# Completing and scaling a softmax sum on VectorE, in front of its reciprocal, in place of GpSimd

## The chip, the cores and the metric

The kernel runs on one core of a Trainium2 chip. A core has TensorE (PE in the profile, with its weight loads as PEld), VectorE (DVE), ScalarE (ACT), GpSimd (POOL) and SyncE (SP), which here only issues transfers. The metric is the device time of one execution in microseconds (us), the median of several runs. The trace is that of one profiled execution, and its times are counted from the start of its span.

## The reference

Attention over 8 batches of 12 heads, 448 positions and 64 features, and then a two-layer network on its output. What is computed:

```python
q_n, k_n = (rmsnorm(q, g_q), rmsnorm(k, g_k))
scores = scale * np.matmul(q_n, k_n.transpose(0, 1, 3, 2))
scores = scores - np.max(scores, axis=-1, keepdims=True)
attn = np.exp(scores)
attn = attn / (np.sum(attn, axis=-1, keepdims=True) + 1e-09)
attn_out = np.matmul(attn, v)
...
x = np.ascontiguousarray(attn_out.transpose(0, 2, 1, 3)).reshape(B * S, H * D)
h = x @ w_in
g = np.where(h > 0.0, h, alpha * (np.exp(np.minimum(h, 0.0)) - 1.0))
return (g @ w_out).astype(np.float32)
```

The network's weights, 768 x 2048 and 2048 x 768, arrive as 64-bit floats.

## The kernel before

**Attention.** Two heads make a pair, and there are 48 pairs. A pair has 7 tiles of 128 query rows (2 x 448 rows), so there are 336 tiles T. A tile goes through these steps: `s_mm` (L488) multiplies queries with keys into one of four PSUM banks; `s_max` (L495, VectorE) takes the negated maximum of each row; `s_exp` (L501, ScalarE) takes the exponential in place and adds the row up, the sum being written by a second, short instruction; `s_z` (L505, GpSimd) adds 1e-9 to the sum and multiplies it by 2^-7; `s_rec` (L512, VectorE) takes its reciprocal; `s_hi` (L516, ScalarE) scales the exponentials and writes them as 16-bit numbers; `s_lo` (L522, VectorE, two instructions) subtracts these from the scaled exponentials and writes what is left as 16-bit numbers too; `s_tr` (L533) issues the transfer that transposes both. Maximum, sum and reciprocal lie side by side in a small tile `st` of 128 x 3, of which there are six. `attend` (L544) multiplies a finished pair with its values into a bank of its own (`av`), and `x_high` and `x_low` (L551, L555) bring the result to SBUF as two 16-bit halves, one 128-row block of the network's input.

**Preparing q, k and v.** Each pair's q and k are loaded, squared (L327), summed (L331), their roots refined on small tiles (L335 to L346), multiplied by them on GpSimd (L356), split into two 16-bit halves (L367 to L388) and transposed by transfers (L396). Values are scaled and split on GpSimd (L402 to L414).

**Weights.** `conv` takes the 64-bit weights apart on the chip: a load (L187), two ScalarE instructions on the upper and lower words (L194, L195), a shift on VectorE (L198), an addition on GpSimd (L204), column sums on TensorE (L115) whose maximum VectorE reads (L118) and turns into powers of two (L124), and a sign put in by VectorE (L223). The first matrix then takes L246 to L260 (GpSimd's part is L249, TensorE's L256 and L257), the second L280 to L292 (GpSimd's are L280 and L289, ScalarE's L285). The first matrix is converted from the start on, the second from half step 60 on. From the eighth piece of the second matrix on its column sums use the bank `av`.

**The network.** `mlp` multiplies a batch by the first matrix (L630), applies the activation (L568 on ScalarE, L571 on GpSimd, L577 on VectorE, and L582 and L585, which split the result into two halves), multiplies by the second (L644), and writes the result out. Every product is made of three 16-bit products.

**The order.** Everything is emitted in half steps h by a loop written out by hand, and each engine runs its instructions in that order. An odd half step has `s_exp(T)`, `s_rec(T-1)` and `s_lo(T-2)`, an even one `s_max(T)`, `s_z(T-1)`, `s_hi(T-2)` and transposes; a table `tasks` adds the other steps at half steps of their own. From half step 92 on (the first batch's 84 and 8 more) 6.9 matrix products of the network are emitted in each half step, between the attention's; up to there TensorE has attention and weights alone. Transfers are all issued from SP's queue in the same order.

Of the kernel before, what the change touches and what calls it, by code (L numbers as in the profile page):

```python
# [14 lines left out]
ALU = mybir.AluOpType  # L15
# [17 lines left out]
def tile_attention_then_elu_mlp(ctx: ExitStack, tc: tile.TileContext, qk, v, v_scan, gg, w_in, w_out, out):  # L33
# [13 lines left out]
    nc = tc.nc  # L47
# [15 lines left out]
    def t_mo():  # L63
# [8 lines left out]
        out=neg, in0=ident, scalar1=-1.0, scalar2=None, op0=ALU.mult  # L72
# [3 lines left out]
        out=ident, in0=ident, scalar1=2.0**UP, scalar2=None, op0=ALU.mult  # L76
# [224 lines left out]
    nat, vn, vt, qkt, pts, pss, p16s, stats = ({} for _ in range(8))  # L301
# [179 lines left out]
    def s_mm(T):  # L481
        p, j = divmod(T, NJ)
        ps = pss[T] = t_s()
        qq = qkt[p].rearrange("p t j n -> p t (j n)")
        for t in (1, 2):
            for h, r0, q0, n in cuts(ORDER[j]):
                lhs = qq[:, 0, h * S + q0 : h * S + q0 + n]
                nc.tensor.matmul(  # L488
                    ps[r0 : r0 + n, :S], lhs, qq[:, t, h * S : h * S + S],
                    start=(t == 1), stop=(t == 2),  # L490
                )

    def s_max(T):
        st = stats[T] = small("st", 3, bufs=6)
        nc.vector.tensor_reduce(  # L495
            out=st[:, 0:1], in_=pss[T][:, :S], axis=AX.X, op=ALU.max, negate=True
        )

    def s_exp(T):
        ps, st = pss[T][:, :S], stats[T]  # L500
        nc.scalar.activation(ps, ps, AF.Exp, bias=st[:, 0:1], accum_out=st[:, 1:2])  # L501

    def s_z(T):
        st = stats[T]
        nc.gpsimd.tensor_scalar(  # L505
            out=st[:, 1:2], in0=st[:, 1:2], scalar1=1e-9, scalar2=2.0**-7, op0=ALU.add, op1=ALU.mult
        )

    def s_rec(T):

        st = stats[T]
        nc.vector.reciprocal(out=st[:, 2:3], in_=st[:, 1:2])  # L512

    def s_hi(T):
        p16 = p16s[T] = pool.tile([128, 2 * S], F16, tag="p16", name="p16", bufs=3)
        nc.scalar.activation(p16[:, :S], pss[T][:, :S], AF.Copy, scale=stats[T][:, 2:3])  # L516

    def s_lo(T):

        p16, ps, r = p16s[T], pss.pop(T), stats.pop(T)[:, 2:3]  # L520
        for o, a, z in ((S + 64, 0, 384), (S, 384, S)):
            nc.vector.scalar_tensor_tensor(  # L522
                out=p16[:, o : o + z - a], in0=ps[:, a:z], scalar=r, in1=p16[:, a:z],
                op0=ALU.mult, op1=ALU.subtract,
            )

    def s_tr(T):
        p, j = divmod(T, NJ)
        p16 = p16s.pop(T)
        for h, r0, q0, n in cuts(ORDER[j]):  # L530
            if 2 * p + h not in pts:
                pts[2 * p + h] = pool.tile([128, NJ, S], F16, tag="pt", name="pt", bufs=2)
            nc.sync.dma_start_transpose(  # L533
                out=pts[2 * p + h][:, :, q0 : q0 + n], in_=p16[r0 : r0 + n, :]
            )

    def attend(p):


        pt = [pts.pop(2 * p), pts.pop(2 * p + 1)]  # L540
        terms = [(j, i) for j in range(4) for i in (0, 1)] + [(j, 0) for j in range(4, NJ)]
        for k, (j, i) in enumerate(terms):
            for h in (0, 1):
                nc.tensor.matmul(  # L544
                    av[64 * h : 64 * h + 64, :S], vt[p][:, j % 4, h, i],
                    pt[h][:, j, :], start=(k == 0), stop=(k == len(terms) - 1),
                )
        del vt[p]
# [109 lines left out]
    def steps_at(h, steps):  # L658
        for i, s in steps:
            at(h + i, s)  # L660

    def run_tasks(h, kind):
        for fn, args in tasks.get(h, []):
            if kind == (0 if fn in (load_qk, load_v, scan_load) else 2 if fn in late else 1):
                fn(*args)
# [54 lines left out]
    for h in range(H0, LAST):  # L720
        T, odd = divmod(h, 2)
        run_tasks(h, 0)
        ok = lambda t: 0 <= t < NCHUNK
        if odd:
            if ok(T):
                s_exp(T)
            if ok(T - 1):
                s_rec(T - 1)
            if ok(T - 2):
                s_lo(T - 2)  # L730
        else:
            if ok(T):
                s_max(T)
            if ok(T - 1):
                s_z(T - 1)
            if ok(T - 2):
                s_hi(T - 2)

            for t in (T - 4, T - 3):
                if ok(t) and (t % NJ == 0) == (t == T - 4):  # L740
                    s_tr(t)
        run_tasks(h, 1)
        want = int(max(0, (h + 1 - START)) * RATE)
        n = max(0, want - done)
        mm = []
        p, r = divmod(h, HP)

        if ok(T + 1) and odd == (h >= START):
            mm.append(lambda: s_mm(T + 1))
        if r == 7 and 0 <= p - 1 < NP:  # L750
            mm = [lambda mm=mm: (*(fn() for fn in mm), attend(p - 1))]
        parts = len(mm) + 1
        for k in range(parts):
            for _ in range(n * (k + 1) // parts - n * k // parts):
                r = next(moe, None)
                done += 1
                if r:
                    steps_at(h + 1, enumerate(r))
            if k < len(mm):
                mm[k]()  # L760
        run_tasks(h, 2)
# [50 lines left out]
```

## Time and profile before

| | us |
|---|---|
| median of 3 runs | 1323.66 (1322.05 to 1326.17) |
| the profiled execution | 1321.52 |
| its span | 1319.7 |
| PE busy | 1202.7 (91%) |
| DVE busy | 897.0 (68%) |
| ACT busy | 820.8 (62%) |
| POOL busy | 672.4 (51%) |
| the sum's completion, L505 on POOL, 336 times | 78.6, 234 ns each on average |
| the reciprocal, L512 on DVE, 336 times | 51.5, 153 ns each on average |

Busy times are those of an engine's own instructions; waiting is not part of them. In a timeline a row gives the start, the duration, the engine, the line, the operation, what it writes and reads, and in square brackets how long the engine had been idle before it and who released it. Consecutive instructions of one engine can overlap a little, as reading, computing and writing are pipelined. In a list of waits a row names who waited, for whom, how long in total, how often, and the longest.

### The profile page before, as it was taken

The page shows a single profiled execution, that of the slowest core. Times are in us where ns is not written, and L with a number is a line of the kernel's source. Part 1 is how long each engine was busy: PE and PEld are TensorE (multiplying, and loading weights), DVE is VectorE, ACT ScalarE, POOL GpSimd, SP SyncE. Part 2 cuts the span into 40 slices and gives each one's busy share as a digit, 9 for nine tenths or more (in the row PEclk, how much of TensorE's full clock was granted, in tenths as well). Part 3 has the DMA queues.
Part 4 walks back from the last instruction along what each step waited for, and adds up shares of the span by engine and source line. Part 5 has one row for each costly group of instructions (what it writes and reads, how often), then busy time and mean ns, then how long its engine had stood idle before and what let it go on. Part 6 is the DMA issues. An engine that isn't in the chain of part 4 may idle for free.

```text
span 1319.7 us, 22020 instructions
## 1 busy us (share of the span) xinstructions
PE 1202.7 (91%) x6976; PEld 723.1 (55%) x6976; DVE 897.0 (68%) x2257; ACT 820.8 (62%) x1761; POOL 672.4 (51%) x915
## 2 busy tenths in 40 slices
PE   3665558879999999999999999999999999999998
PEld 1322224436755675566655765577556755666576
DVE  7776788988668756885588657865687568842310
ACT  5767767776667657675577657756676567742310
POOL 5776798888445544544455345543454445421100
PEclk9777768989999999999999999999999999999999
DMA  7899998879878787888878877879687877764011
GB/s 236 195 233 223 201 203 189 209 205 204 199 140 194 163 187 151 178 165 189 173 153 177 190 172 147 187 171 193 144 190 163 189 150 154 152 135 110 1 46 60
DMA packets 491013, 221.76 MB, mean 168 GB/s; under 512 B 451856, under 2 KB 467344, under 8 KB 490896
## 3 DMA queue, kind: packets, MB, share of 16 engines
q1 hardware_dynamic: 490896, 220.35, 75.6%
q8 instruction: 55, 0.90, 0.3%
q14 instruction: 62, 0.51, 0.1%
HBM read 96.01 MB, written 14.16 MB: 83 GB/s over the span
## 4 chain that ended last, share of the span: by engine, by line
PE 67%; DMA 4%; DVE 4%; POOL 2%; issue 2%; ACT 2%; SPq 0%; ACTq 0%; POOLq 0%
PE mo L644 32%; PE mo L630 22%; PE s L488 7%; PE av L544 6%; DMA pt<-p 2%; DMA vscan<-in_v_scan 1%; DVE p L522 1%; POOL e L571 1%; POOL t L381 1%; DVE st L495 1%; DVE mv L139 0%; DVE e L577 0%; ACT p L516 0%; DVE wts L198 0%; ACT t L367 0%
## 5 line engine op out<-in xcount | busy, mean ns | idle before, releaser
L630 PE MATMUL mo<-x,whi 128*128 128x448 f16 x1536 | 425.8, 354 | 1.5 <-DVE e L577 1.5
L644 PE MATMUL mo<-g,who 128*128 128x448 f16 x1536 | 422.5, 352 | 0.0
L495 DVE TENSOR_REDUCE st<-s 128x1 f32<-128x448 f32 x336 | 208.1, 619 | 205.5 <-PE s L488 205.3
L522 DVE SCALAR_TENSOR_TENSOR p<-s,st,p 128x384 f16<-128x384 f32 (+1 forms) x672 | 266.4, 437 | 34.7 <-ACT p L516 33.2
L516 ACT ACTIVATE p<-s,st 128x448 f16<-128x448 f32 x336 | 213.1, 634 | 120.7 <-DMA pt<-p 95.3
L644 PE MATMUL mo<-g,wls 128*128 128x448 f16 x768 | 272.0, 354 | 0.0
L630 PE MATMUL mo<-x,wli 128*128 128x448 f16 x768 | 271.8, 354 | 0.0
L644 PEld LDWEIGHTS <-who 128*128 128x128 f16 x1536 | 221.9, 144 | 72.3
L505 POOL TENSOR_SCALAR st<-st 128x1 f32<-128x1 f32 x336 | 78.6, 234 | 350.7 <-ACT s L501 333.5
L501 ACT ACTIVATE s<-s,st 128x448 f32<-128x448 f32 x336 | 203.8, 607 | 74.0 <-DVE st L495 64.6
L488 PE MATMUL s<-qkt 128*128 128x448 f16 (+1 forms) x768 | 191.4, 372 | 58.9 <-DVE p L522 30.7
L630 PEld LDWEIGHTS <-whi 128*128 128x128 f16 x1536 | 150.6, 98 | 139.6 <-issue 4.4
L571 POOL TENSOR_SCALAR e<-e,isc 128x448 f32<-128x448 f32 x128 | 94.1, 735 | 179.5 <-ACT e L568 177.7
L644 PEld LDWEIGHTS <-wls 128*128 128x128 f16 x768 | 111.5, 145 | 42.1 <-issue 7.5
L488 PEld LDWEIGHTS <-qkt 128*128 128x128 f16 (+1 forms) x768 | 61.3, 102 | 131.6 <-DVE p L522 52.2
L544 PE MATMUL av<-pt,vt 128*64 128x448 f16 x1056 | 114.6, 366 | 5.2 <-DVE mx L118 4.3
L585 DVE SCALAR_TENSOR_TENSOR g<-e,gsc,g 128x448 f16<-128x448 f32 x128 | 100.8, 788 | 24.4 <-ACT g L582 24.3
L630 PEld LDWEIGHTS <-wli 128*128 128x128 f16 x768 | 75.2, 98 | 74.5 <-issue 8.1
L582 ACT ACTIVATE g<-e,gsc 128x448 f16<-128x448 f32 x128 | 85.4, 667 | 44.9 <-DVE e L577 44.1
L568 ACT ACTIVATE e<-mo,sc 128x448 f32<-128x448 f32 x128 | 80.4, 628 | 52.3 <-PE mo L630 33.1
L381 POOL TENSOR_TENSOR t<-nat,t 128x896 f16<-128x896 f32 x48 | 92.7, 1931 | 4.8 <-ACT t L367 1.1
L577 DVE SCALAR_TENSOR_TENSOR e<-e,mo 128x448 f32<-128x448 f32 x128 | 78.2, 611 | 23.9 <-POOL e L571 19.3
(84 smaller groups left out, 1330.0 us busy)
## 6 DMA issues: line engine op xcount, KB each, us to landing
wls<-wl_d SPq DMA_DIRECT2D x48, 512.0 KB, 3.9
nat<-in_qk SPq DMA_DIRECT2D x48, 448.0 KB, 3.7
raws<-in_w_in SPq DMA_DIRECT2D x16, 768.0 KB, 5.5
vn<-in_v SPq DMA_DIRECT2D x48, 256.0 KB, 3.7
raws<-in_w_out SPq DMA_DIRECT2D x24, 512.0 KB, 4.2
vscan<-in_v_scan SPq DMA_DIRECT2D x48, 224.0 KB, 3.0
out<-y SPq DMA_DIRECT2D x48, 224.0 KB, 3.2
pt<-p SPq DMA_TRANSPOSE x384, 3.2
```

Source lines behind the costliest of these rows:

```text
L381: nc.gpsimd.tensor_tensor(out=t[:, 2], in0=twice(nat[p][:, 1]), in1=t[:, 1], op=ALU.subtract)
L488: nc.tensor.matmul(ps[r0 : r0 + n, :S], lhs, qq[:, t, h * S : h * S + S], start=(t == 1), stop=(t == 2),)
L495: nc.vector.tensor_reduce(out=st[:, 0:1], in_=pss[T][:, :S], axis=AX.X, op=ALU.max, negate=True)
L501: nc.scalar.activation(ps, ps, AF.Exp, bias=st[:, 0:1], accum_out=st[:, 1:2])
L516: nc.scalar.activation(p16[:, :S], pss[T][:, :S], AF.Copy, scale=stats[T][:, 2:3])
L522: nc.vector.scalar_tensor_tensor(out=p16[:, o : o + z - a], in0=ps[:, a:z], scalar=r, in1=p16[:, a:z], op0=ALU.mult, op1=ALU.subtract,)
L544: nc.tensor.matmul(av[64 * h : 64 * h + 64, :S], vt[p][:, j % 4, h, i], pt[h][:, j, :], start=(k == 0), stop=(k == len(terms) - 1),)
L571: nc.gpsimd.tensor_scalar(out=e, in0=e, scalar1=-1.0, scalar2=isc, op0=ALU.add, op1=ALU.mult)
L582: nc.scalar.activation(g[:, 0], e, AF.Copy, scale=gsc)
L585: nc.vector.scalar_tensor_tensor(out=g[:, 1], in0=e, scalar=gsc, in1=g[:, 0], op0=ALU.mult, op1=ALU.subtract)
L630: nc.tensor.matmul(ph[:, :S], w[:, c, :], x[:, r, :], start=(c == 0 and i == 0), stop=last)
L644: nc.tensor.matmul(py[:, :S], w, g[:, r, :], start=(f == 0 and i == 0), stop=last)
```

## The change

The completion of the sum goes from GpSimd to VectorE, into the function that takes the reciprocal, and directly in front of it; `s_z` and its call are gone. The arithmetic, its constants and its operands are the same. Within the order the instruction thus moves from the even half step of its tile to the odd one behind it, after `s_exp(T)` has been emitted and ahead of `s_lo(T-2)`.

```diff
-    def s_z(T):
+    def s_rec(T):
+
         st = stats[T]
-        nc.gpsimd.tensor_scalar(
+        nc.vector.tensor_scalar(
             out=st[:, 1:2], in0=st[:, 1:2], scalar1=1e-9, scalar2=2.0**-7, op0=ALU.add, op1=ALU.mult
         )
-
-    def s_rec(T):
-
-        st = stats[T]
         nc.vector.reciprocal(out=st[:, 2:3], in_=st[:, 1:2])
...
             if ok(T):
                 s_max(T)
-            if ok(T - 1):
-                s_z(T - 1)
             if ok(T - 2):
                 s_hi(T - 2)
```

## Prediction

> **What bounds the kernel now.** I read the windows first, because a mean over 1.3 ms would mix stages with different limits. The columns are stage, its length, then busy microseconds (and instructions) of PE, PEld, DVE, ACT and POOL, then the granted TensorE clock, the DMA share and GB/s.
>
> ```profile
> 0.00:145.00 145.00, 82.86 (x466) 40.70 (x468) 106.82 (x264) 100.61 (x212) 102.20 (x105) 0.80 0.86 215
> 145.00:198.00 53.00, 24.79 (x162) 10.47 (x157) 42.63 (x111) 37.32 (x82) 45.30 (x50) 0.65 0.96 215
> 198.00:315.00 117.00, 100.86 (x637) 54.49 (x635) 104.63 (x246) 85.18 (x177) 98.44 (x110) 0.93 0.84 201
> 315.00:1197.00 882.00, 875.09 (x5081) 540.87 (x5080) 621.92 (x1605) 572.49 (x1252) 414.62 (x631) 1.00 0.81 170
> ```
>
> From 315 us on PE is busy 875.09 of 882 us: that stage, and the matmuls left after 1197 us, last as long as their matmuls whatever DVE and POOL do. Ahead of it no engine is full. PE is busy 82.86 of 145, then 24.79 of 53, then 100.86 of 117 us, while DVE and POOL both stand between 70% and 90%. So the change is worth something, or costs something, in the first 315 us only, and how much is read from who waits for whom there. The waits of the first 300 us and of the rest (engine and line that waits, whom for, total us, times, longest):
>
> ```profile
> POOL st L505 <- ACT s L501: 19.5, 13, 4.1
> ...
> DVE st L512 <- POOL st L505: 15.9, 16, 3.4
> ```
>
> ```profile
> DVE st L495 <- PE s L488: 203.9, 181, 1.8
> ```
>
> L505 is the instruction that moves (I call it z), L512 the reciprocal, L495 the row maximum. Early on POOL stands 19.5 us in front of z until ScalarE has summed the exponentials, and DVE stands 15.9 us in front of the reciprocal until POOL has done z. After 300 us DVE stands 203.9 us waiting for new scores. How many z there are in the later stages (busy us, count):
>
> ```profile
> 145.00:198.00 53.00, 2.76 (x14) 0.65 0.96 215
> 198.00:315.00 117.00, 7.62 (x26) 0.93 0.84 201
> 315.00:1197.00 882.00, 58.55 (x264) 1.00 0.81 170
> ```
>
> **The change part by part.** *What is added on DVE:* one instruction per tile, tensor_scalar of 128x1 to 128x1 f32 with two immediates. The trace has no z on DVE; its nearest row is L124, the same operation, shape and engine with integers, and two of those in a row, the second reading what the first wrote, show the step when one depends on the other, as the reciprocal does on z:
>
> ```profile
> L124 DVE TENSOR_SCALAR ws<-mx x24: 153/154/156, 152.6 to 323.5; 128x1 int32<-128x1 int32 x24
> ```
>
> ```profile
> 112.19 0.15 DVE L124 TENSOR_SCALAR p<-mx 128x1 int32<-128x1 int32 x1
> 112.38 0.15 DVE L124 TENSOR_SCALAR vs<-p 128x1 int32<-128x1 int32 x1
> ```
>
> A z lasts 0.154 us and holds up what depends on it by 112.38 − 112.19 = 0.19 us. That is the value I take. The lower bound is 0.08 us, the step from a reciprocal to an instruction that does not need it (137.87 to 137.95, below). The upper bound is the same operation on a wide tile, DVE's shift L198, whose mean is far above what it needs:
>
> ```profile
> L198 DVE TENSOR_SCALAR wts<-wts 128x512 int32<-128x512 int32 x24 | 21.1, 879 | 0.4 <-ACT wts L194 0.2
> ```
>
> It takes 0.42 us at 151.44 (below) and 0.879 us on average, 0.46 us more, which I put down to POOL's instructions running at the same time; 0.19 + 0.46 = 0.65 us. I stay at 0.19, because L124's 24 rows lie between 153 and 156 ns from 152.6 to 323.5 us, where POOL is busiest. Below nothing it cannot go: DVE does strictly more.
>
> The Trainium skill, page "SBUF — State Buffer", section "SBUF: two separate sides", gives a mechanism for the upper bound: a DVE instruction in a two-port mode and a GpSimd instruction take a shared port pair as an exclusive lock for the whole instruction, and the loser blocks. Taken for every instruction from SBUF to SBUF with one source, it would catch z as it catches the shift, and the result would be the third rival's; 153 to 156 ns for one element per partition speaks against that.
>
> *The wait that is added:* z on DVE waits for ScalarE's sum of tile T−1. Behind it in DVE's queue stand the reciprocal and the two subtractions of tile T−2 (L522), and for those PE's next scores and the transposes wait. But the subtractions need ScalarE's scaled copy of tile T−2 (L516), which stands behind that same sum in ScalarE's queue. So the new wait always ends before the wait that stands right behind it already, and I cost it at nothing; if ScalarE's order were otherwise, each such wait would be worth some of the 15.9 us.
>
> *What is removed:* z on POOL, with the step to the next instruction 152.16 − 151.88 = 0.28 us (below), POOL's wait in front of it, and DVE's wait on POOL. No DMA moves with it and no queue is passed by one: SP's order is unchanged.
>
> After 315 us z adds 0.19 us to 264 tiles, 50 us, all of it under the 203.9 us in which DVE waits for scores; without that cover it would cost those 50 us. There I count 0.
>
> *0 to 145 us.* The work comes in periods of seven tiles. The path through one, in DVE's rows and then PE's, of which the first is the same wait a period earlier:
>
> ```profile
> 135.87 0.62 DVE L495 TENSOR_REDUCE st<-s 128x1 f32<-128x448 f32 x1 [0.33 <-PE s L488]
> ...
> 137.87 0.15 DVE L512 RECIPROCAL st<-st 128x1 f32<-128x1 f32 x1
> 137.95 0.79 DVE L522 SCALAR_TENSOR_TENSOR p<-s,st,p 128x384 f16<-128x384 f32 x2
> ```
>
> ```profile
> 111.55 0.69 PE L488 MATMUL s<-qkt 128*64 128x448 f16 x4 [2.55 <-DVE p L522]
> ...
> 138.79 0.62 PE L488 MATMUL s<-qkt 128*64 128x448 f16 x4 [2.55 <-DVE p L522]
> ```
>
> PE delivers scores, DVE takes their maximum at 135.87 and runs without a gap to the subtractions at 137.95, and PE, which stood 2.55 us for them, goes on at 138.79 without a gap to the values of the pair, whose end releases transposes and loads. One z falls on that path, in front of 137.87. The other six I put where DVE waits anyway, for ScalarE, PE or a load, and for the same reason I count none of the 15.9 us that DVE stood behind POOL as a gain here: what it wins is lost at its next wait. A period is 138.79 − 111.55 = 27.2 us; from 25 to 145 us there are 4.4: 4.4 × 0.19 = +0.8 us.
>
> *145 to 171 us.* Here w_out is being converted and POOL has more to do. POOL's rows, then DVE's, then PE's:
>
> ```profile
> 148.09 1.15 POOL L414 TENSOR_TENSOR vt<-vn,vt 128x512 f16<-128x512 f32 x1
> 151.88 0.19 POOL L505 TENSOR_SCALAR st<-st 128x1 f32<-128x1 f32 x1 [2.65 <-ACT s L501]
> 152.16 1.69 POOL L356 TENSOR_TENSOR nat<-nat,r 128x896 f32<-128x896 f32 x1
> 153.80 1.26 POOL L204 TENSOR_TENSOR w32s<-wts,w32s 128x512 int32<-128x512 int32 x1
> ...
> 158.73 0.19 POOL L505 TENSOR_SCALAR st<-st 128x1 f32<-128x1 f32 x1 [0.57 <-ACT s L501]
> ```
>
> ```profile
> 151.44 0.42 DVE L198 TENSOR_SCALAR wts<-wts 128x512 int32<-128x512 int32 x1
> ...
> 155.10 0.69 DVE L223 SCALAR_TENSOR_TENSOR w32s<-raws,w32s 128x512 uint32<-128x512 uint32 x1 [1.03 <-POOL w32s L204]
> 156.57 0.16 DVE L512 RECIPROCAL st<-st 128x1 f32<-128x1 f32 x1 [0.78 <-POOL st L505]
> ```
>
> ```profile
> 157.52 0.93 PE L488 MATMUL s<-qkt 128*128 128x448 f16 x2 [3.00 <-ACT wts L194]
> ```
>
> POOL is free at 149.24 and stands 2.65 us in front of z; the normalisation behind it (L356) could have run. Without z it starts at about 149.3 and ends at 151.0; the addition L204 then waits only for DVE's shift, which ends at 151.86, or 0.2 us later if L356 gets in its way. L204 starts at 152.05, not 153.80: 1.75 us earlier. DVE stood 1.03 us for that L204 at 155.10 and 0.78 us for the next z at 156.57, and the subtractions right behind that reciprocal are what PE, idle 3.00 us, got at 157.52. The z at 158.73 held POOL another 0.57 us. Gain 1.75 + 0.57 = 2.3, less two z on DVE's path, 0.4: −1.9 us.
>
> *171 to 198 us.* In this stretch, most of the second window above, POOL (45.30 of 53 us) and DVE (42.63) pace each other. Five tiles: POOL loses 5 × 0.28 = 1.4 us, DVE gains 5 × 0.19 = 0.95 us, and each waits for the other: −0.4 us.
>
> *198 to 315 us.* The chain that ended last runs through the second half of this stage; of it (start, duration, what):
>
> ```profile
> 270.52 1.09 issue
> ...
> 271.65 0.40 POOL st L505
> ...
> 277.75 0.15 DVE st L512
> ...
> 316.75 0.15 DVE st L512
> ```
>
> Seven reciprocals stand on it between 277.75 and 316.75: 7 × 0.19 = +1.3 us. POOL's z stands on it once, 0.40 us with 1.09 us of waiting ahead of it: −1.5 us. Net −0.2 in the 46 us from 270.52 to 316.75; for the whole 117 us I take twice that, −0.4.
>
> The sum is 0.8 − 1.9 − 0.4 − 0.4 = −1.9 us. The profiled execution took 1321.52 us, so it would take 1319.6. It lies 2.1 us below the median of the runs shown, 1323.66; against that median the forecast is 1321.8 us. The runs shown spread over 0.3%, 4 us, and a difference below that can't be told from none.
>
> **The rivals.** *POOL is the pace of 145 to 315 us throughout (faster).* Then all 14 + 26 = 40 z there come off the path: 40 × 0.28 = −11.2 us, 1312.5 us. For it: POOL's 45.30 of 53 us, and the gap of 2.65 us in front of z. Against it: DVE's 104.63 of 117 us, and a chain with seven of DVE's reciprocals to one of POOL's z.
>
> *DVE is the pace of 198 to 315 us (slower).* Its place is DVE's queue between two reads of the bank that PE waits for. It decides once DVE's 117 − 104.63 = 12.4 us of idle time there does not fall behind the z. All 26 z then lie on the path, +4.9 us, with the +0.8 of the first stage, and the gain at 152 us is lost behind DVE again: +5.7 us, 1329.4 us. For it: the seven reciprocals on the chain. Against it: POOL ends its instructions sooner, and DVE waits for those too.
>
> *z on DVE is held up by POOL (slower).* At 0.46 us more, the shift's excess, in the 40 tiles of 145 to 315 us, and half of it on the path: +9.2 on the −1.9, +7.3 us, 1331.0 us. The rows of L124 speak against it.
>
> That the change does not do what it says has no room here: the order is written out by hand, and the instruction goes from one engine to another.
>
> **How the numbers follow.** The forecast has 0.55, POOL's pace 0.26, DVE's pace 0.13, the held-up z 0.06. The likeliest case's own range is 1317.5 to 1325.5: its terms are small, but a shift of a microsecond in the start-up changes which transfers meet. The range with the rivals is 1311.5 to 1329.5, which takes in POOL's pace at 1312.5 and DVE's at 1329.4, and leaves out the held-up z and the far ends of the others. Faster by over 0.3% (below 1319.7): POOL's pace and 0.07 of the forecast's own spread, 0.33. Slower by over 0.3% (above 1327.6): the two slow rivals less 0.02 for milder forms of them, 0.17. Within: 0.50.
>
> **What would show it.** In the profile after: DVE has 336 instructions more and POOL 336 fewer; the new instruction lasts about 154 ns at its median and not over 0.2 us anywhere near POOL; DVE's waits for POOL in front of the reciprocal are gone, and in their place stand shorter ones for ScalarE; POOL runs L356 near 150 us without standing for ScalarE; from about 313 us on PE is full. It is wrong if PE loses time after 315 us, if the new instruction's mean is far above 0.154 us, or if the stage before PE fills becomes more than 5 us longer or shorter.

## The result, and the profile after

| | before | after |
|---|---|---|
| median, us | 1325.75 (1322.05 to 1326.17, 5 runs) | 1331.29 (1329.94 to 1333.51, 5 runs) |
| ratio to before | | 1.0052, 95% interval 1.0034 to 1.0069 |
| the profiled execution, its span | 1321.52, 1319.7 | 1331.29, 1329.4 |
| VectorE busy | 897.0 (68%) | 970.6 (73%) |
| GpSimd busy | 672.4 (51%) | 585.9 (44%) |

The kernel became half a per cent slower, some 7 us (the means of the five runs are 1324.7 and 1331.7 us; the medians of so few runs lie closer together), where I had forecast 1.9 us (0.14%) faster. In the kernel after, lines behind z have moved up by three: z is L506, the reciprocal L509, `s_hi` L513, `s_lo` L519, `attend` L541. The windows that the forecast started from, now of the kernel after, in the same columns:

```profile
0.00:145.00 145.00, 81.58 (x456) 40.65 (x457) 108.79 (x294) 100.49 (x212) 91.99 (x73) 0.80 0.89 215
145.00:198.00 53.00, 25.60 (x168) 11.02 (x166) 45.76 (x127) 37.52 (x81) 39.60 (x36) 0.62 0.92 210
198.00:315.00 117.00, 99.38 (x627) 52.90 (x624) 109.49 (x269) 83.56 (x173) 90.19 (x82) 0.92 0.81 196
315.00:1197.00 882.00, 870.07 (x5046) 535.96 (x5045) 679.82 (x1852) 572.34 (x1248) 352.32 (x368) 1.00 0.81 169
```

Up to 315 us TensorE has been busy 2 us less than before (206.6 for 208.5). From 315 us on it is busy 870.07 us where it was busy 875.09: most of the loss lies in the stage that I had called full. Two `attend` show the same (start, duration). First the one at 389 us and the last one, of before, then the same two of after:

```profile
388.65 2.25 PE L544 MATMUL av<-pt,vt 128*64 128x448 f16 x22
```

```profile
1204.00 2.27 PE L544 MATMUL av<-pt,vt 128*64 128x448 f16 x22
```

```profile
391.13 2.25 PE L541 MATMUL av<-pt,vt 128*64 128x448 f16 x22
```

```profile
1213.68 2.27 PE L541 MATMUL av<-pt,vt 128*64 128x448 f16 x22
```

Between the two lie 815.35 us before and 822.55 us after: 7.2 of the 9.7 us by which the profiled spans differ. The other 2.5 us lie ahead of them, and there single executions differ by more: before and a kernel further down, first halves, have the same order up to the `attend` ahead of these, and it comes at 365.48 us in the one and at 369.74 in the other. What TensorE waits for there, from 330 to 1320 us, of before and then of after (total us, times, longest):

```profile
PE av L544 <- DVE mx L118: 4.3, 4, 1.5
PE av L544 <- DMA pt<-p: 0.8, 1, 0.8
```

```profile
PE av L541 <- DVE mx L118: 5.3, 5, 1.3
PE av L541 <- DMA pt<-p: 4.5, 5, 1.3
```

`attend` now waits 4.5 us for the transposes of its pair, where it waited 0.8: 3.7 of the 7.2 us, and the other row adds 1.0. VectorE's groups show why it may come late (busy us, mean ns of one, then the idle time ahead of them). Of after, and then the one row of before that the forecast had not looked at:

```profile
L509 DVE RECIPROCAL st<-st 128x1 f32<-128x1 f32 x336 | 55.1, 164 | 11.5
L372 DVE TENSOR_TENSOR nat<-nat,gst 128x448 f32<-128x448 f32 x42 | 48.8, 1162 | 0.0
L506 DVE TENSOR_SCALAR st<-st 128x1 f32<-128x1 f32 x336 | 48.5, 144 | 1.4 <-ACT s L501 1.2
```

```profile
L372 DVE TENSOR_TENSOR nat<-nat,gst 128x448 f32<-128x448 f32 x42 | 28.2, 672 | 0.0
```

z is as cheap as forecast, 144 ns, and waits 1.2 us for ScalarE in all; the reciprocal takes 164 ns for 153. But `q_gain` (L372), the product of a pair's queries with their gain, on which nothing was changed, has gone from 672 to 1162 ns: 20.6 us more of VectorE in 42 instructions. That is the row to read in this profile. One of them, in the first half of a batch (while the network's first matrix is multiplied), in the kernel before, on VectorE and then on GpSimd:

```profile
685.38 0.67 DVE L372 TENSOR_TENSOR nat<-nat,gst 128x448 f32<-128x448 f32 x1
```

```profile
687.46 0.55 POOL L505 TENSOR_SCALAR st<-st 128x1 f32<-128x1 f32 x1 [1.88 <-ACT s L501]
688.08 1.89 POOL L381 TENSOR_TENSOR t<-nat,t 128x896 f16<-128x896 f32 x1
```

And the same pair in the kernel after, GpSimd and then VectorE:

```profile
688.01 0.64 POOL L568 TENSOR_SCALAR e<-e,isc 128x448 f32<-128x448 f32 x1 [2.16 <-ACT e L565]
688.61 1.89 POOL L381 TENSOR_TENSOR t<-nat,t 128x896 f16<-128x896 f32 x1
```

```profile
688.74 2.25 DVE L372 TENSOR_TENSOR nat<-nat,gst 128x448 f32<-128x448 f32 x1
690.90 0.14 DVE L506 TENSOR_SCALAR st<-st 128x1 f32<-128x1 f32 x1
691.08 0.16 DVE L509 RECIPROCAL st<-st 128x1 f32<-128x1 f32 x1
```

L381 is `k_low`, a subtraction on GpSimd that reads two operands from SBUF. In the kernel before it stands in GpSimd's queue behind the z of the tile before, and that z waits 1.88 us for ScalarE; so `q_gain` is over at 686.05 and `k_low` starts at 688.08. In the kernel after no z stands there, `k_low` goes straight behind an instruction of the activation (L568), at 688.61, and `q_gain` arrives 0.13 us behind it. It lasts 2.25 us: the 1.76 us for which `k_low` still runs, and 0.49 us. It is the same elsewhere: from 330 us on all 36 `k_low` of before stand directly behind a z; of those of after 18 go straight behind an L568, and the other 18 go as soon as ScalarE has made their input, for which they stand ready (total us, times, longest):

```profile
POOL t L381 <- ACT t L367: 148.2, 18, 10.9
```

22 of the 36 `q_gain` then start while a `k_low` runs. The chain that ended last goes through this one instruction (start, duration, what):

```profile
688.82 2.16 DVE nat L372
690.98 0.07 DVE st L506
...
691.16 0.81 DVE p L519 x2
...
694.84 3.59 DMA pt<-p
...
698.56 2.24 PE av L541 x21
```

`q_gain` holds up z and the reciprocal, these the subtraction, that the transpose, and that `attend`, for which TensorE stands still. In the kernel before the chain is on TensorE itself at this place.

### The profile page after: what moved, and what is told of

Same layout as the page of the kernel before. It is cut to its first block, busy times and chain, and to the rows that moved or that the text cites. A ratio compares the mean times of both kernels' runs of the same rounds, so it can differ in the third digit from the quotient of the medians.

```text
span 1329.4 us, 22012 instructions
## 1 busy us (share of the span) xinstructions
PE 1205.4 (91%) x6976; PEld 724.3 (54%) x6976; DVE 970.6 (73%) x2593; ACT 823.6 (62%) x1761; POOL 585.9 (44%) x579
## 4 chain that ended last, share of the span: by engine, by line
PE 63%; DVE 9%; DMA 5%; ACT 1%; issue 1%; SPq 1%; ACTq 0%
PE mo L641 32%; PE mo L627 19%; PE av L541 6%; PE s L488 6%; DMA pt<-p 5%; DVE p L519 2%; DVE g L582 2%; DVE st L495 1%; DVE e L574 1%; DVE nat L372 1%; ACT p L513 1%; DVE wts L198 1%; DVE ss L331 1%; DVE w32s L223 0%; DVE mv L139 0%
## 5 line engine op out<-in xcount | busy, mean ns | idle before, releaser
L495 DVE TENSOR_REDUCE st<-s 128x1 f32<-128x448 f32 x336 | 208.5, 621 | 165.1 <-PE s L488 164.2
L513 ACT ACTIVATE p<-s,st 128x448 f16<-128x448 f32 x336 | 212.5, 632 | 132.1 <-DMA pt<-p 93.4
L519 DVE SCALAR_TENSOR_TENSOR p<-s,st,p 128x384 f16<-128x384 f32 (+1 forms) x672 | 271.7, 446 | 30.9 <-ACT p L513 29.8
L568 POOL TENSOR_SCALAR e<-e,isc 128x448 f32<-128x448 f32 x128 | 86.8, 678 | 330.0 <-ACT e L565 285.1
L381 POOL TENSOR_TENSOR t<-nat,t 128x896 f16<-128x896 f32 x48 | 95.1, 1981 | 150.4 <-ACT t L367 150.4
L541 PE MATMUL av<-pt,vt 128*64 128x448 f16 x1056 | 116.8, 367 | 9.9 <-DVE mx L118 5.3
L582 DVE SCALAR_TENSOR_TENSOR g<-e,gsc,g 128x448 f16<-128x448 f32 x128 | 103.5, 808 | 23.4 <-ACT g L579 23.3
L356 POOL TENSOR_TENSOR nat<-nat,r 128x896 f32<-128x896 f32 (+1 forms) x48 | 84.4, 1758 | 54.0 <-DVE st L506 46.3
L541 PEld LDWEIGHTS <-vt 128*64 128x64 f16 x1056 | 66.1, 114 | 52.3 <-issue 19.5
```

The lines of the kernel that those rows point to most:

```text
L381: nc.gpsimd.tensor_tensor(out=t[:, 2], in0=twice(nat[p][:, 1]), in1=t[:, 1], op=ALU.subtract)
L495: nc.vector.tensor_reduce(out=st[:, 0:1], in_=pss[T][:, :S], axis=AX.X, op=ALU.max, negate=True)
L519: nc.vector.scalar_tensor_tensor(out=p16[:, o : o + z - a], in0=ps[:, a:z], scalar=r, in1=p16[:, a:z], op0=ALU.mult, op1=ALU.subtract,)
L541: nc.tensor.matmul(av[64 * h : 64 * h + 64, :S], vt[p][:, j % 4, h, i], pt[h][:, j, :], start=(k == 0), stop=(k == len(terms) - 1),)
L568: nc.gpsimd.tensor_scalar(out=e, in0=e, scalar1=-1.0, scalar2=isc, op0=ALU.add, op1=ALU.mult)
L582: nc.vector.scalar_tensor_tensor(out=g[:, 1], in0=e, scalar=gsc, in1=g[:, 0], op0=ALU.mult, op1=ALU.subtract)
```

## The experiments

Ratios are to the kernel before, run beside each on the same chip; 0.1% is 1.3 us. Of each kernel the mean of its `q_gain` in the profile is given.

| kernel | z on GpSimd | z on VectorE | `q_gain`, ns | median, us | ratio, 95% interval |
|---|---|---|---|---|---|
| before | yes | | 672 | 1323.9, 1324.1, 1322.5 | 1 |
| after, again | | yes | 1150 | 1331.1 | 1.0055 (1.0037 to 1.0073) |
| no z (e1_fold) | | | 1168 | 1321.5 | 0.998 (0.9971 to 0.999) |
| both (e2_both) | yes | yes | 690 | 1333.7 | 1.0069 (1.0057 to 1.0081) |
| start only (e5_start) | later | start | 703 | 1323.2 | 0.9992 (0.9982 to 1.0002) |
| first halves (e6_first) | else | first halves | 812 | 1329.7 | 1.0041 (1.0028 to 1.0055) |
| after, early (e12_early) | | yes | 704 | 1323.7 | 0.9994 (0.9984 to 1.0004) |
| no z, early (e13_fold_early) | | | 650 | 1315.2 | 0.993 (0.9914 to 0.9945) |
| tether (e10_tether) | unread | yes | 690 | 1334.9 | 1.0076 (1.0061 to 1.0091) |
| after, moved (e8_relief) | | yes | on GpSimd | 1323.5 | 0.9991 (0.9981 to 1.0001) |
| no z, moved (e9_fold_relief) | | | on GpSimd | 1314.6 | 0.9933 (0.992 to 0.9945) |
| before, early (e14_before_early) | yes | | 683 | 1322.7 | 1.0003 (0.999 to 1.0016) |
| before, late (e16_before_late) | yes | | 1293 | 1341.9 | 1.0134 (1.0117 to 1.0152) |

**First round: is it z's time on VectorE?** The first theory, D, was that VectorE has no time to spare in the first half of each batch, so that z's own steps there cost what the mean over the stage hid. Its rival P was that the loss comes from GpSimd's side, from what is gone there. Four kernels had z on no engine, on both, and on VectorE in some places only.

No z at all: the factor 2^7 goes into the power of two by which the values are scaled, and the 1e-9 is left out.

```diff
-        nc.vector.tensor_scalar(
-            out=st[:, 1:2], in0=st[:, 1:2], scalar1=1e-9, scalar2=2.0**-7, op0=ALU.add, op1=ALU.mult
-        )
         nc.vector.reciprocal(out=st[:, 2:3], in_=st[:, 1:2])
...
-            ibits(vs, p2, -1, ALU.mult, (254 + 7 + UP) * E, ALU.add)
+            ibits(vs, p2, -1, ALU.mult, (254 + 14 + UP) * E, ALU.add)
```

> No z on any engine: the reciprocal is taken of the plain sum, the factor 2^7 that this drops is put into the power of two by which the values are scaled, and the 1e-9, below the last bit of a sum that is at least 1, is left out. Theory D (DVE has no time to spare in the start-up and in the first half of each batch, and z's own time on DVE is what costs): the time is that of the kernel before or a little less, ratio 0.996 to 1.000, and PE loses nothing more around 700, 840 and 980 us than before. Rival P (it is taking z away from POOL, which changes when POOL runs its other work, or the reciprocal's waiting for ScalarE directly, that costs): the time is that of the changed kernel, ratio 1.004 to 1.006.

Both: GpSimd's z stays, and VectorE copies its result to a fourth column with the same operation (0 added, times 1) ahead of the reciprocal.

```diff
-        nc.vector.reciprocal(out=st[:, 2:3], in_=st[:, 1:2])
+        nc.vector.tensor_scalar(
+            out=st[:, 3:4], in0=st[:, 1:2], scalar1=0.0, scalar2=1.0, op0=ALU.add, op1=ALU.mult
+        )
+        nc.vector.reciprocal(out=st[:, 2:3], in_=st[:, 3:4])
```

> z stays on POOL as before, and DVE does an instruction of z's kind beside it (adds 0, multiplies by 1) between POOL's z and the reciprocal. Theory D: as slow as the changed kernel, ratio 1.004 to 1.008, with PE's losses at the same places (around 420, 560, 700, 840 and 980 us). Rival P: as fast as the kernel before, 0.999 to 1.001.

z on VectorE for T < 88 alone (the start), or from tile 88 on in the first 24 of each 42 tiles alone (the first halves of the batches); elsewhere on GpSimd.

```diff
+    def on_dve(T):
+        return T < 88            # e6_first: T >= 88 and (T - 4) % 42 < 24
     def s_z(T):
+        if on_dve(T):
+            return
...
     def s_rec(T):
+        if on_dve(T):
+            nc.vector.tensor_scalar(...)
```

> z on DVE for the first 88 tiles only, on POOL for the others. The changed kernel was 2.5 us behind when PE became full (at about 320 us). Theory D and the even spread both expect about that: +2.5 us, ratio 1.001 to 1.003, and no loss after 330 us.

> z on DVE only after tile 88, in the 24 tiles of each batch in which the network's first matrix is multiplied (T-4 modulo 42 below 24), on POOL for all others. Theory D: all of the late loss is here, +6 to +7 us, ratio 1.0045 to 1.0055. Even spread over the tiles (a cost per z wherever it stands): 24 of 42 of it, +4 us, ratio 1.003.

By their times alone these four spoke more for D than for P. A z added on VectorE cost 0.69% (both, to before) and, with none on GpSimd, 0.72% (after, to no z); GpSimd's z cost only 0.2%; the exchange in the first halves alone cost 0.41%, a little below D's band, which its interval reaches. That in the start alone cost nothing, 0.9992 (0.9982 to 1.0002), where 1.001 to 1.003 had been expected: a miss. But the profiles did not fit: no z has almost the same late loss as after, with nothing added on VectorE: 821.69 us between the same two `attend`, for 822.55 in after and 815.35 in before. The row that D had no place for is `q_gain`'s. From 330 us on, in no z, both and first halves (minimum, median and maximum in ns):

```profile
L372 DVE TENSOR_TENSOR nat<-nat,gst x35: 607/1115/2276, 351.0 to 1151.4; 128x448 f32<-128x448 f32 x35
```

```profile
L372 DVE TENSOR_TENSOR nat<-nat,gst x36: 609/615/1002, 342.3 to 1163.6; 128x448 f32<-128x448 f32 x36
```

```profile
L372 DVE TENSOR_TENSOR nat<-nat,gst x36: 612/615/2280, 339.5 to 1162.9; 128x448 f32<-128x448 f32 x36
```

Where GpSimd has its z, a `q_gain` takes 615 ns; where it has none, typically 1115 and up to 2276. In first halves only a few are hit, but by the full 2.28 us. So theory C, which is P with the instructions named: the z on GpSimd waited for ScalarE, and this wait kept `k_low` behind `q_gain`. By C no z had lost to collisions most of what it gained, and that GpSimd's z seemed cheap, and VectorE's dear, came from the same thing.

**Second round: the collision by itself.** In after and in no z, `q_gain` of pairs 7 on goes one tile earlier in the order, where its input has long been there and `k_low`'s has not:

```diff
-        steps = (-20, -12, -10, -8, -6, -2, 1, 2, 4, 4, 6)
+        steps = (-20, -12, -10, -8, -6, -2, 1, 0 if p > NPAIR else 2, 4, 4, 6)
```

> The kernel after, with q_gain of pairs 7 on put one tile earlier in the order (half-step 0 in place of 2), so that it is done before k_low of its pair can start on GpSimd. Theory D (VectorE has too much to do in the first half of each batch, z's own steps are the cost): about as after, 1330 to 1332 us, since the same instructions stand on VectorE. Theory C (without z, GpSimd no longer waits for ScalarE, its subtraction k_low runs while q_gain is on VectorE and q_gain takes 1.2 to 2.3 us in place of 0.61): q_gain back at 0.61 us in nearly all of its 42, 20 us of VectorE and ScalarE's waits gone, 1323 to 1326 us.

> The fold (no z on any engine, 1e-9 left out) with q_gain of pairs 7 on one tile earlier. D: as the fold, 1321 to 1322 us. C: the fold had the same collisions (q_gain 1.17 us in the mean), which hid some of what it gains; 1314 to 1318 us, with the wait of attend for its transposes gone.

C, both times. After, early is back at before's time, 0.9994, with every instruction of after still there (six `q_gain` still take 1.0 us, beside an L568, none runs beside a `k_low`); no z, early is the fastest so far, 0.993. The last `attend` of after, early starts 817.78 us behind the one at 388.37, 4.8 us less than in after. Its rows at 388 and 1206 us, its waits, and the two instructions apart:

```profile
388.37 2.25 PE L541 MATMUL av<-pt,vt 128*64 128x448 f16 x22
```

```profile
1206.15 2.27 PE L541 MATMUL av<-pt,vt 128*64 128x448 f16 x22
```

```profile
PE av L541 <- DMA pt<-p: 1.6, 2, 1.0
```

```profile
682.99 0.76 DVE L372 TENSOR_TENSOR nat<-nat,gst 128x448 f32<-128x448 f32 x1
```

```profile
685.89 1.89 POOL L381 TENSOR_TENSOR t<-nat,t 128x896 f16<-128x896 f32 x1
```

The next kernel was meant to put GpSimd's wait back and nothing else: z on VectorE, and at its old place GpSimd does the same operation into a column that nothing reads.

```diff
     def s_z(T):
         nc.gpsimd.tensor_scalar(
-            out=st[:, 1:2], in0=st[:, 1:2], scalar1=1e-9, scalar2=2.0**-7, op0=ALU.add, op1=ALU.mult
+            out=st[:, 3:4], in0=st[:, 1:2], scalar1=1e-9, scalar2=2.0**-7, op0=ALU.add, op1=ALU.mult
```

> z on VectorE, and at its old place GpSimd keeps the same operation on the same operand, with its result written to a column that nothing reads. GpSimd waits for ScalarE as before, but nothing waits for GpSimd. D: VectorE's work is that of after, GpSimd's that of before; 1331 to 1334 us, like the kernel with both. C: q_gain at 0.61 to 0.69 us, and 1325 to 1329 us.

Here C missed. The collisions are gone, 690 ns, and the kernel is slower than after, 1.0076. But it does not leave VectorE free, as I had assumed: VectorE's z overwrites the column that GpSimd's z reads, so it has to come behind it. Its waits (L512 here; total us, times, longest):

```profile
DVE st L512 <- POOL st L505: 11.0, 15, 1.4
```

In the kernel both, the same line has the same wait, 11.0 us in 15 times, and the two kernels take about the same time, 1.0076 and 1.0069. So this one is a second case of both, and no test of GpSimd's wait alone; what that wait would cost is not shown. What the two show is that a second z has a price without any collision.

The collision can be removed in another way, with `q_gain` on GpSimd too, in `k_low`'s own queue:

```diff
-        eng = nc.gpsimd if 0 < p <= NPAIR else nc.vector
+        eng = nc.gpsimd if p else nc.vector
```

> The kernel after, with q_gain of pairs 7 on moved to GpSimd (1.25 to 1.5 us each there for 0.6 to 2.3 on VectorE). Both theories expect a gain: D by 0.61 us a pair taken from VectorE against 7 z of 0.25 (about a third of the 9 us back, 1327 to 1329); C by that and the collisions too (1322 to 1326). If GpSimd's 1.3 us come late for q_high on ScalarE, slower than after.

0.9991, within C's band and below D's.

**Third round: the controls.** The same early `q_gain` in the kernel before, a late one there (half step 4, where z has just let `k_low` go), no z with `q_gain` on GpSimd, and after once more.

> The kernel before with q_gain of pairs 7 on one tile earlier: the control for the same move in the kernel after. Theory C (the move gains only by keeping q_gain and k_low apart): before has no such collisions after 330 us (q_gain 0.61 us in nearly all), so 1323 to 1325 us, ratio within 0.1% of 1. Rival E (an earlier q_gain is better by itself, because q_high and the transposes come earlier): about 7 us faster, 1316 to 1318.

> The kernel before with q_gain of pairs 7 on one tile later (half-step 4 in place of 2), where GpSimd, let go by z, starts k_low. z stays on GpSimd. C: q_gain takes 1.2 to 2.3 us in the mean in most pairs, and the kernel loses what after lost, 4 to 9 us: 1328 to 1333 (q_gain that ends later is part of it, as it was in after). D (only z's own steps on VectorE cost): 1323 to 1326.

> The fold (no z on any engine, 1e-9 left out) with q_gain of pairs 7 on moved to GpSimd. C: collisions gone, 1314 to 1318 us, as the fold with the early q_gain; VectorE's 28 us less bring at most a microsecond or two more. D: 1318 to 1320.

> The kernel after once more, beside the controls on one chip: ratio 1.004 to 1.007 to before, q_gain 1.1 to 1.2 us in the mean.

The early place brings the kernel before nothing, 1.0003: it gains only where there is a collision to remove. The late place makes the collisions with z still on GpSimd (row below, from 330 us on, against 615 in before), and the kernel loses 1.34%. That is the direction that C gives, but about twice its upper bound: here the later `q_gain` also makes what waits for it late (ScalarE stands 61.9 us, in 30 times, for it in front of `q_high`), and this kernel can't tell the two apart.

```profile
L372 DVE TENSOR_TENSOR nat<-nat,gst x36: 615/1442/2325, 340.9 to 1174.0; 128x448 f32<-128x448 f32 x36
```

No z with `q_gain` on GpSimd is as fast as no z, early: VectorE's 27 us less bring nothing that shows (0.9933 against 0.993). After, again gives 1.0055 for the 1.0052 of the first measurement.

**The account.** The kernels in which no `q_gain` meets a `k_low` give the price of a z by itself, the others that of the collisions (differences of ratios, times 1324 us):

- z on GpSimd: before less no z, early, 1 − 0.993 = 0.70%, 9.3 us.
- z on VectorE: after, early less no z, early, 0.9994 − 0.993 = 0.64%, 8.5 us.
- the exchange without collisions: −0.06%, −0.8 us (interval −2.1 to +0.5).
- collisions: after less after, early, 1.0052 − 0.9994 = 0.58%, 7.7 us; with no z, 0.998 − 0.993 = 0.50%, 6.6 us.
- both z and no collisions: 0.993 + 0.0070 + 0.0064 = 1.0064; measured 1.0069 and, with the unread one, 1.0076.
- first halves: 0.41%, 5.4 us, with four collisions of 2.24 to 2.28 us and no other.

So the exchange of engines is worth nothing that can be measured, and the loss is the collisions. Few of them reach TensorE as such a wait. In after, four of the five times that TensorE stands for transposes (556.9, 698.6, 840.2 and 981.6 us, 4.2 of the 4.5 us) come some 10 us behind a `q_gain` of 2.25 us in the first half of a batch; behind the other 18 there is none. The kernel first halves has only four collisions, all of that kind; TensorE stands 3.0 us behind three of them, and its late loss is that of after, 822.62 us between the two `attend`. The rest of the 7.7 us was not followed to single collisions.

Where a z has its price can be read too, in one profile of each kernel. The `attend` at 389 us comes at 382.4 to 384.9 us in the three kernels without z, at 388.3 to 392.9 in the nine with one, on either engine, and at 396.1 and 397.6 in the two with both. Most of the price thus lies in the first 390 us. Which waits make it up was not tried and stays open.

## Why the prediction was wrong

**The step that failed** is "*What is removed*", and with it the "There I count 0" for the time after 315 us, where 7.2 us were lost (one profile of each). The step lists "z on POOL, with the step to the next instruction", "POOL's wait in front of it, and DVE's wait on POOL", and every one of them is priced as a gain. That wait was also what kept everything behind z in GpSimd's queue from starting sooner. I checked that "SP's order is unchanged" and that no transfer passes a queue; the order within each queue is indeed the same, but the order in time between two queues is not. The forecast used this in the one place where it helped, at 152 us ("the normalisation behind it (L356) could have run"), and did not ask it of L381 and L388 in the other 1000 us. GpSimd's wait in front of z there, 314.0 us in all, stood first in the list of waits after 300 us from which the forecast took its 203.9 us:

```profile
POOL st L505 <- ACT s L501: 314.0, 166, 4.6
```

The early `q_gain` shows this step as the cause: with it the kernel runs at 0.9994, −0.8 us, and the forecast's −1.9 us lies in that interval.

**"From 315 us on … last as long as their matmuls whatever DVE and POOL do"** fell with it. 203.9 us of waiting for scores is a sum over all that comes after 300 us; behind the `q_gain` at 688.74 us VectorE ran without a gap to the subtraction, had none of it to give, and 1.6 us more on one instruction arrived at TensorE as 1.21 us of standing still. Without `k_low`'s collisions the step holds better: from the `attend` at 389 us to the last one, after, early has 817.78 us, after, moved (which also frees VectorE of `q_gain`) 814.89 and before 815.35, so z by itself comes to between −0.5 and +2.4 us where I counted 0 (one profile of each). "If PE loses time after 315 us" was the forecast's own sign of being wrong.

**The third rival** had the mechanism and the wrong victim. I let GpSimd hold up z and turned it down by L124's 153 to 156 ns; z was indeed never held up, 130 to 155 ns in all 336. Its +7.3 us is near the measured 7 by chance. The Trainium skill, page "SBUF — State Buffer", section "SBUF: two separate sides", counts among the VectorE instructions that need the shared port pair those "with two SBUF inputs (only against a GpSimd op that reads SBUF)". The trace agrees: `q_gain` reads two operands from SBUF and took 2.25 us beside `k_low`, and z reads one and took 0.14. I had weighed that rule against the instruction that moves, and not against the instructions that stay and get a new neighbour.

**What held.** z's duration (154 ns forecast, 144 measured). Its dependent step: 690.90 to 691.08, 0.18 us, for 0.19. The new wait on ScalarE "at nothing": 1.2 us in 5 waits. The start: the exchange there alone gives 0.9992, −1.1 us (interval −2.4 to +0.3), for a sum of −1.9 over the first 315 us; the sign can't be told. Nor is it shown that its four terms were right: a z costs several us there on either engine (above), far more than any of the terms, and that the two prices cancel is more than the forecast knew. That its sum fits may be luck. The two rivals on who paces 145 to 315 us did not show: in that kernel POOL's pace would have been 11 us faster, DVE's pace 6 us slower.

## What to carry to other kernels

A wait that is taken off an engine lets the engine's next instructions run earlier, and these have neighbours: list what stands behind it in the queue, and what the other engines do at the new time, before calling the wait a gain. After any move, compare the mean duration of the instructions that were not touched; a group whose mean changes though its code did not (672 to 1162 ns here) is a collision, and times of kernels with and without the moved part alone had pointed to the wrong cause. A single instruction that is not needed can be folded away on whichever engine it stands: no z with an early `q_gain` takes 1315.2 us, 0.70% less than the kernel before.

## What the runs showed of the hardware that I had not expected

The hold-up works in both directions and for the whole instruction. In after, 22 `q_gain` started while a `k_low` ran, and every one ended 0.48 to 0.49 us after it. In before, at 403 us, VectorE's product came first, and GpSimd's instruction behind it took 0.96 us, for a median of 0.64: VectorE's product ended 0.45 us after its start, and it 0.51 us later.

```profile
403.64 0.61 DVE L372 TENSOR_TENSOR nat<-nat,gst 128x448 f32<-128x448 f32 x1
```

```profile
403.80 0.96 POOL L571 TENSOR_SCALAR e<-e,isc 128x448 f32<-128x448 f32 x1 [1.15 <-ACT e L568]
```

VectorE's instructions that read a PSUM bank or one small operand were not slowed beside the same `k_low`. In after, 26 row maxima (L495) lie wholly within a `k_low`, at 612 to 626 ns for a median of 624, and 32 instructions of `s_lo`, at 274 to 277 and 617 to 618 ns for medians of 276 and 618. And the price of the collisions is not their length: 20.6 us more of VectorE cost 7.7 us, and in first halves 5.9 us more cost 5.4.
